# Softmax tiles on VectorE, taken in pairs instead of one at a time

## Chip, cores, metric

The kernel runs on one core of a Trainium2 chip. The metric is the device time of one execution in microseconds (us). ScalarE is called ACT in the profile, VectorE DVE, TensorE PE (its weight loads PEld), GpSimd POOL, SyncE (which issues the DMAs) SP.

## What is computed

Two layers of the same transformer block are run one after the other on x of 2048 rows and 448 columns (bf16); both layers share their weights.

```python
def _A_ref(x, wqkv, wo):
    B, S, D = x.shape
    H = 16; Dh = D // H
    ...                                   # q, k, v of x @ wqkv
    scores = jnp.einsum("bhqd,bhkd->bhqk", q, k) * scale
    p = _softmax(scores, axis=-1)
    o = jnp.einsum("bhqk,bhkd->bhqd", p, v)
    return ... @ wo
def _B_ref(x, w1, b1, w2, b2):
    h = jnp.einsum("bsd,df->bsf", x, w1) + b1
    r = jnp.where(h > zero, h, zero)
    out = jnp.einsum("bsf,fd->bsd", r * r, w2) + b2
x = A_x
x = x + _A_ref(_layernorm(x), A_wqkv, A_wo)
x = x + _B_ref(_layernorm(x), B_w1, B_b1, B_w2, B_b2)
...                                       # the same two lines once more
```

There are 16 heads of width 28 and an MLP of width 1792 with a squared ReLU. The exponentials of the scores, 2 x 16 x 2048 x 2048 of them, are the largest single piece of elementwise work.

## The kernel before

**Tiles.** The rows are cut into blocks of 256 queries (the last two of the second layer have 128). A *pass* is one block and one group of four heads; it runs over the keys in pieces. A *unit* is 512 columns of scores of one head (128 keys on the partitions, 2 x 256 or 4 x 128 columns). There are 2048 units. `s_stream` takes three units at a time as a *group*: PE computes their scores into a PSUM tile `sc` of 1536 columns (two such buffers), L817. `e_stream` lets ScalarE take exp of the tile into `pt` (bf16, NPT = 11 buffers), L842. `p_stream` multiplies `pt` with the values, L1000, and accumulates a pass in one PSUM bank; after it come the softmax division, the output projection, the layer norm and the MLP of the block (`chain`), which are interleaved with the passes of later blocks. Evictions of all these products (L1184, L1191, L1136, L580, L576 and others) run on VectorE, L1242 is filling work for PE.

**Order.** Nothing is scheduled by the chip or a compiler here: a `Planner` with a clock for each engine and an estimated duration for each operation runs generators ("streams") with priorities, always takes the operation that can start earliest, and emits the instructions in that order. Each engine then runs its instructions in the order of emission and waits for semaphores.

**VectorE's share of the exponentials.** For some groups, `apart` decides that VectorE computes the exponential of one of the three units. Then ScalarE's instruction has only 1024 columns. VectorE's way takes five instructions on 512 columns, in a *set* of work tiles:

- L900: scores (PSUM) to a whole number in fixed point (`i`), a scale and a clamp; after it, and after ScalarE, the score buffer is free;
- L916: from the upper half words of `i`, the power of two (`e`);
- L923: from the lower half words and `e`, the first factor, into `e`;
- L928: from the lower half words, the second factor, into `h`;
- L938: their product, into a bf16 tile `pd` that PE reads like `pt`.

There are two sets (`R_v`): the tiles v_i, v_e, v_h, and room in the keys buffer `K_sb` of the other layer (there `h` lies in `i`, so that L928 must wait for L923). The second set is used where that buffer is idle: blocks 2 to 6 in the first layer, all of the second. The `pd` tiles come from `R_pd` (`pd_free`): a tile of its own, idle room in `V_sb`, and, late, NHP buffers of the pool `h`.

`apart` gives a unit to VectorE only if a set is free, `pd` tiles are left, the scores' inputs are there, VectorE was booked for no more than BUSY of the last SPAN = 6 us, and the tile work not yet booked (`left`, 2.74 for one tile) with VectorE's backlog is at most TB us:

```python
if pl.load(SPAN, "DVE") > (LOW if behind(i) else BUSY):
    return None
if max(0.0, pl.clock["DVE"] - now) + left[0] > (TB2 if behind(i) else TB):
    return None
```

`behind(i)` says whether the MLP work is late against a straight line (constants L0E, L0N, L1E, L1N, MARGIN); then the smaller limits LOW and TB2 hold. STOP = 80: none of the last 80 units is given to VectorE. The first step of a tile has a high priority (C_PRIO), the other four (`a_rest`) a low one (V_PRIO, V_LATE, V_LAST as the tile ages), behind the evictions (EV).

Of the kernel before, what the change touches and what calls it, by code (L numbers as in the profile page):

```python
# [18 lines left out]
G = 4  # L19
# [11 lines left out]
OVER = 0.08  # L31
QUICK = 0
QUICK3 = 2
# [7 lines left out]
HALF = 320  # L41
L0E = 1310
L0N = 7.8
L1E = 2020
L1N = 6.6
MARGIN = 4.0
LOW = 0.95
# [10 lines left out]
AHEAD = (range(0, 4), range(0, 4), range(0, 4), range(0, 1))  # L58
SLACK = 0.5
WINDOW = 2.8  # L60
C_PRIO = 1.6
V_PRIO = 8.0
V_LATE = 4.6
V_LAST = 3
V_AGE = 8
V_PAST = 4
OWN3 = 0
FIRST = 50
V_FIRST = 9
V_WAIT = 3.5  # L70
NEAR = 6
FAR = 17
KEEP = 5
LAG = 7
LEAD = 15
LAST = 690
BUSY = 1.0
TB = 4.8
TB2 = 0.3
SPAN = 6  # L80
# [4 lines left out]
MORE = 3  # L85
HEAT = 0.76
HWIN = 3.4
# [3 lines left out]
HOLD1 = 7  # L91
SOON = 0
NHP = 3
THIRD = 1
NL = 0
NLP = 4.9
STOP = 80
HSTOP = 0
CHUNK = 2
EV = 2.9  # L100
CUTS = (0, 10, 16)
# [124 lines left out]
def kernel(  # L226
# [466 lines left out]
    def behind(i):  # L693
# [3 lines left out]
        return done[l] < (min(i, b) - a) / (b - a) * n * per[l] - MARGIN  # L697
    pending = [0]
    left = [0.0]

# [7 lines left out]

    def apart(i, now, us, soon=SOON):

        if len(units) - i < STOP or not LEAD <= len(gbuf) <= LAST:
            return None
        l, qb = passes[units[i][0]][:2]
        if sum(r.when() is not None and r.when() <= now + soon for r in sets_of(units[i])) <= (0 if soon else pending[0]):
            return None
        j = i
        if i + LAG > ends_at[units[i][0]]:
            j = ends_at[units[i][0]] + 1
            while j in taken:
                j += 1  # L720
            if j >= len(units):
                return None
            rows = {u[3] for u in us}
            js = [k for k in range(j, j + 4) if k < len(units) and k not in taken and units[k][3] not in rows]
            j = js[0] if js else j
        if passes[units[j][0]][0] != passes[us[0][0]][0]:
            return None
        if held[0] + 1 > min(sum(r.n for r in pd_free(units[k])) for k in (i, j)):
            return None
        if any(pl.tok.get(d) is None or pl.tok[d].end + LAT["DVE"] > now for d in needs(units[j])):  # L730
            return None
        if pl.load(SPAN, "DVE") > (LOW if behind(i) else BUSY):
            return None
        if max(0.0, pl.clock["DVE"] - now) + left[0] > (TB2 if behind(i) else TB):
            return None
        return j
# [16 lines left out]
    def s_stream():  # L753
        while at[0] < len(units):
# [5 lines left out]
            def fn(e, gi=gi, us=us, js=js):  # L760
# [5 lines left out]
                def next_at(j):  # L766
# [3 lines left out]
                    return rest  # L770
                own, j = True, None
                if OWN3 and bank_free(o.start) and next_at(js[-1] + 1):
                    j = apart(at[0], o.start, us)
                elif len(us) == 3 and THIRD:
                    own = False
                    next_at(js[1] + 1)
                    j = apart(at[0], o.start, us[:2], 0.0)
                if j is None:
                    next_at(js[-1] + 1)
                else:  # L780
                    if not own:
                        us, ks = us[:2], ks[:2]
                        gbuf[gi]["n"] = 2
                    us, ks = us + [units[j]], ks + [3]
                    taken.add(j)
                    held[0] += 1
                    pending[0] += 1
                    next_at(at[0])
                    if own:
                        x = gbuf[gi]["x"] = Op("PE", 0.0, None)  # L790
                        x.res = min((r for r in R_m if r.when() is not None), key=lambda r: r.when())
                        x.turn = len(x.res.rel)
                        x.res.rel.append(None)
                        dst.append(bank(x, "mt"))
                    else:
                        x = gbuf[gi]["x"] = o
                        o.need = 2
                    pl.spawn(C_PRIO, a_unit(gi, x, dst[-1], us[-1], passes[us[0][0]][0]))
                for k, (pi, kb, r, hh) in zip(ks, us):
# [72 lines left out]

    v_i = const.tile([P, 512], DT.int32, name="v_i")
    v_e = const.tile([P, 512], DT.int32, name="v_e")
    v_h = const.tile([P, 512], DT.float32, name="v_h")

    def set_of(res, l):

        k = R_v.index(res)
        two = lambda a: a.rearrange("p (a n) -> p a n", a=2)  # L880
        if k == 0:
            i, e, h = two(v_i[:, :]), two(v_e[:, :]), two(v_h[:, :])
        else:
            keys = K_sb[1 - l][:, :, S - 512:S] if l == 0 else K_sb[0][:, :, 0:512]
            i, e = keys[:, 0:2, :].bitcast(DT.int32), keys[:, 2:4, :].bitcast(DT.int32)
            h = i.bitcast(DT.float32)
        return i, e, h, two

    def a_unit(gi, x, src, unit, l):
        yield Op("-", 0.0, None, deps=[("s", gi)])  # L890
        box = {}

        def take(e):
            pending[0] -= 1
            box["i"], box["e"], box["h"], two = set_of(c.res, l)
            box["two"] = two
            halves = box["i"].bitcast(DT.uint16).rearrange("p a (n t) -> p a n t", t=2)
            box["f"] = halves[:, :, :, 0]
            box["n"] = box["i"].bitcast(DT.int16).rearrange("p a (n t) -> p a n t", t=2)[:, :, :, 1]
            t = nc.vector.tensor_scalar(out=box["i"], in0=two(src), scalar1=EXP_BIAS,  # L900
                                        scalar2=EXP_LOW, op0=ALU.add, op1=ALU.max)
            if x is gbuf[gi]["s"]:
                apart_from(gi, t)
        c = Op("DVE", 0.69, take, deps=[("s", gi)], acq=sets_of(unit), rel=x)
        left[0] += 2.74
        yield c
        left[0] -= 0.6
        pl.spawn(lambda now: V_LAST if e_now[1] - gi >= V_AGE or at[0] > ends_at[unit[0]] + V_PAST else V_LATE if now > c.end + V_WAIT else V_PRIO if gi > FIRST else V_FIRST, a_rest(gi, c, box, unit))

    def a_rest(gi, c, box, unit):  # L910

        root, lin, low = EXP_POLY
        flt = lambda k: box[k].bitcast(DT.float32)

        def power(e):
            nc.vector.tensor_scalar(out=box["e"], in0=box["n"], scalar1=2.0 ** 22, scalar2=EXP_BASE,  # L916
                                    op0=ALU.mult, op1=ALU.add)
        p = Op("DVE", 0.42, power, deps=[c])
        yield p
        left[0] -= 0.34  # L920

        def first(e):
            nc.vector.scalar_tensor_tensor(out=flt("e"), in0=box["f"], scalar=root, in1=flt("e"),  # L923
                                           op0=ALU.add, op1=ALU.mult)
        g = Op("DVE", 0.684, first, deps=[p])

        def square(e):
            nc.vector.scalar_tensor_tensor(out=box["h"], in0=box["f"], scalar=lin, in1=box["f"],  # L928
                                           op0=ALU.add, op1=ALU.mult)
        alone = c.res is R_v[0]  # L930
        h = Op("DVE", 0.684, square, deps=[c] if alone else [c, g])
        for k in (h, g) if alone else (g, h):
            yield k
            left[0] -= 0.6

        def close(e):
            pd = gbuf[gi]["pd"] = pd_of(o)
            nc.vector.scalar_tensor_tensor(out=box["two"](pd), in0=box["h"], scalar=low, in1=flt("e"),  # L938
                                           op0=ALU.add, op1=ALU.mult)
        o = Op("DVE", 0.683, close, deps=[g, h], acq=lambda: pd_free(unit), rel=c, sets=("x", gi))  # L940
        gbuf[gi]["x"] = o
        yield o
        left[0] -= 0.6

# [5 lines left out]
    def p_stream():  # L950


        for pi, (l, qb, g, kbs, first, last) in enumerate(passes):
# [18 lines left out]
            while todo:  # L972
                now = [kb for kb in todo if done(kb)][:some]
                if len(now) < min(some, len(todo)):
                    kb = next(kb for kb in todo if not done(kb))
                    if ("u", pi, kb) not in pl.tok or any(k < 3 and ("e", gi) not in pl.tok for gi, k, _ in where[pi, kb]):
                        yield from got(kb)
                        continue
                    if (e_now[1] - min(gi for gi, _, _ in where[pi, kb]) < NPT - KEEP and e_now[1] < len(gbuf) - 1
                            and len(todo) > len(now) + 1):  # L980
                        yield Op("-", 0.0, None, deps=[("e", e_now[1] + 1)])
                        continue

                    now = sorted(now[:some - 1] + [kb])
                    yield Op("-", 0.0, None, deps=[("x", gi) for gi, k, _ in where[pi, kb] if k == 3])
                todo = [kb for kb in todo if kb not in now]
# [30 lines left out]
            def ev(e, box=box, first=first, last=last, g=g, res=res, n=n, l=l, qb=qb):  # L1017
# [5 lines left out]
                else:  # L1023
                    dst = part(l, qb, g)
                if first:
                    nc.vector.tensor_copy(out=dst, in_=src)
# [266 lines left out]
```

## Time and profile before

| | |
|---|---|
| median of 8 runs | 875.2 us (874.33 to 876.95) |
| profiled execution | 875.5 us, its span 873.7 us |
| ACT, DVE, PE busy | 857.2, 824.0, 828.1 us |
| granted PE clock | 1.000 |
| groups of exponentials on ACT | 509 of 1536 columns, 174 of 1024 |
| tiles on VectorE | 173: 98 in v_i, 75 in K_sb |

The page of the profile lists engines with their busy time, the share of the span and the number of instructions. A row of a group reads: line, engine, operation, out<-in with the shapes, count, then busy time and mean length of one in ns, then the engine's idle time just before these instructions and who ended it. A row of the waits reads: who waited, for whom, us in total, times, longest. A row of the timeline reads: start, length, engine, line, operation. A row of a stretch gives the length, then the busy times of PE, PEld, DVE, ACT and POOL with their instructions, the granted clock, the DMAs' share and GB/s. The instructions of an engine overlap slightly, so that lengths add up to more than the busy time.

### The profile page before, as it was taken

What the parts mean: (1) busy time and instruction counts of PE and PEld (TensorE: products, weight loads), DVE (VectorE), ACT (ScalarE), POOL (GpSimd) and SP (SyncE); (2) the same over time, 40 slices, a digit from 0 to 9 for tenths busy, and PEclk for the clock granted to TensorE, in tenths of its full rate; (3) what the DMA queues carried; (4) which work ended last, traced back from release to release, by engine and by line L of the source; (5) the groups of instructions that cost most, each with busy time, mean ns of one, the idle gap of its engine ahead of it and who ended that gap; (6) DMA issues with size and microseconds to landing.
All of it is one profiled execution on the core that took longest, in us unless ns stands there. A gap on an engine that the chain in (4) does not pass through costs nothing.

```text
span 873.7 us, 28872 instructions
## 1 busy us (share of the span) xinstructions
PE 828.1 (95%) x12673; PEld 445.2 (51%) x12673; DVE 824.0 (94%) x1685; ACT 857.2 (98%) x702; POOL 45.4 (5%) x95
## 2 busy tenths in 40 slices
PE   8999999999999999999999999999999999999998
PEld 5455554454545555454545544444454554545656
DVE  7999899999999999998989999999999999999954
ACT  8999999999999999999999999999999999999995
POOL 3100000001000000100000000000000000000000
DMA  9100100000000000000000000010000000000000
GB/s 256 52 2 3 25 17 15 14 15 15 7 10 15 14 15 15 2 15 14 2 3 2 2 3 2 16 28 27 23 17 26 14 26 25 11 17 15 14 8 18
DMA packets 31514, 17.86 MB, mean 20 GB/s; under 512 B 17242, under 2 KB 30939, under 8 KB 31388
## 3 DMA queue, kind: packets, MB, share of 16 engines
q1 hardware_dynamic: 31388, 16.02, 6.5%
q8 instruction: 99, 1.62, 0.7%
q14 instruction: 27, 0.22, 0.1%
HBM read 13.73 MB, written 2.06 MB: 18 GB/s over the span
## 4 chain that ended last, share of the span: by engine, by line
ACT 59%; PE 19%; issue 10%; DVE 10%; POOL 0%; DMA 0%; DVEq 0%; ACTq 0%
ACT pt L842 59%; PE mt L558 8%; PE sc L817 6%; PE oT L1000 3%; DVE K_sb L923 1%; PE sc L558 1%; DVE r L1184 1%; PE mt L1242 1%; DVE K_sb L928 1%; DVE v_h L928 1%; DVE K_sb L900 1%; DVE v_i L900 1%; DVE x_sb L1136 1%; PE mt L340 1%; DVE v_e L923 1%
## 5 line engine op out<-in xcount | busy, mean ns | idle before, releaser
L842 ACT ACTIVATE pt<-sc 128x1536 bf16<-128x1536 f32 (+1 forms) x683 | 844.9, 1480 | 3.3 <-PE sc L817 3.0
L817 PE MATMUL sc<-Q_sb,K_sb 32*128 32x256 bf16 (+1 forms) x5660 | 317.2, 265 | 32.6 <-ACT pt L842 28.3
L817 PEld LDWEIGHTS <-K_sb 32*128 32x128 bf16 x5660 | 144.1, 92 | 213.3 <-issue 177.1
L1000 PE MATMUL oT<-pt,V_sb 128*32 128x256 bf16 (+1 forms) x3994 | 152.9, 268 | 0.2
L558 PE MATMUL mt<-xnT,w 128*128 128x256 bf16 (+1 forms) x912 | 121.6, 270 | 2.4 <-DVE r L1184 0.7
L1000 PEld LDWEIGHTS <-V_sb 128*32 128x32 bf16 x4352 | 90.9, 96 | 47.4 <-issue 44.6
L558 PEld LDWEIGHTS <-w 128*128 128x128 bf16 x952 | 77.6, 98 | 39.9 <-issue 31.4
L1184 DVE TENSOR_SCALAR r<-mt 128x512 bf16<-128x512 f32 x107 | 72.8, 681 | 5.1 <-PE mt L558 4.8
L900 DVE TENSOR_SCALAR v_i<-sc 128x512 int32<-128x512 f32 x98 | 66.8, 681 | 4.3 <-PE sc L817 3.8
L558 PE MATMUL mt<-w,V_sb 128*128 128x448 bf16 (+1 forms) x288 | 68.1, 348 | 0.0
L928 DVE SCALAR_TENSOR_TENSOR v_h<-v_i 128x512 f32<-128x512 uint16 x98 | 66.5, 678 | 0.0
L923 DVE SCALAR_TENSOR_TENSOR v_e<-v_i,v_e 128x512 f32<-128x512 uint16 x98 | 66.3, 677 | 0.0
L1242 PE MATMUL mt<-xn,ident 128*128 128x448 bf16 x176 | 60.2, 356 | 1.8 <-DVE oTn L1085 0.5
L475 POOL TENSOR_TENSOR ve<-mv,eps_t 128x2 f32<-128x2 f32 (+1 forms) x34 | 13.0, 383 | 814.5 <-DVE mv L453 814.5
L900 DVE TENSOR_SCALAR K_sb<-sc 128x512 int32<-128x512 f32 x75 | 51.1, 682 | 1.9 <-PE sc L817 1.4
L923 DVE SCALAR_TENSOR_TENSOR K_sb<-K_sb 128x512 f32<-128x512 uint16 x75 | 51.3, 683 | 0.8
L928 DVE SCALAR_TENSOR_TENSOR K_sb<-K_sb 128x512 f32<-128x512 uint16 x75 | 50.9, 679 | 0.5
L1136 DVE TENSOR_TENSOR x_sb<-x_sb,mt 128x448 bf16<-128x448 bf16 (+1 forms) x63 | 38.0, 604 | 10.1 <-PE mt L558 9.8
L916 DVE TENSOR_SCALAR v_e<-v_i 128x512 int32<-128x512 int16 x98 | 40.7, 415 | 0.3
L448 DVE BATCH_NORM_STATS2 st<-x_sb 128x6 f32<-128x448 bf16 x64 | 39.0, 612 | 0.7 <-DMA x_sb<-in_A_x_dram 0.7
L558 PEld LDWEIGHTS <-V_sb 128*128 128x128 bf16 x302 | 25.3, 98 | 25.6 <-issue 10.5
L938 DVE SCALAR_TENSOR_TENSOR V_sb<-v_h,v_e 128x512 bf16<-128x512 f32 x55 | 37.4, 680 | 0.2
(102 smaller groups left out, 802.3 us busy)
## 6 DMA issues: line engine op xcount, KB each, us to landing
rec<-scr SPq DMA_DIRECT2D x54, 128.0 KB
x_sb<-in_A_x_dram SPq DMA_DIRECT2D x8, 224.0 KB
out_dram<-x_sb SPq DMA_DIRECT2D x15, 112.0 KB
w<-in_B_w_dram SPq DMA_DIRECT2D x1, 1568.0 KB
w<-in_B_w_dram SPq DMA_DIRECT2D x1, 1344.0 KB
dn<-oT_sb SPq DMA_DIRECT2D x54, 4.0 KB
V_sb<-in_A_wqkv_dram SPq DMA_DIRECT2D x4, 168.0 KB
scr<-dn SPq DMA_DIRECT2D x27, 8.0 KB
```

The lines of the kernel that those rows point to most:

```text
L448: nc.vector.bn_stats(out=box["st"][:, :], in_=x_sb[:, t0 + j, :])
L558: nc.tensor.matmul(box["t"][:, c0:c0 + n], lhsT=lhsT() if callable(lhsT) else lhsT, rhs=rhs, start=a, stop=b)
L817: nc.tensor.matmul(dst[k][:, i * nt * P:(i + 1) * nt * P], lhsT=K_sb[l][rows, g, (kb + i) * P:(kb + i + 1) * P], rhs=Q_sb[rows, g, t0 * P: ...
L842: t = nc.scalar.activation(out=pt[:, 0:n], in_=gbuf[gi]["sc"][:, 0:n], func=AF.Exp, scale=float(np.log(2.0)) * 2.0 ** -FRAC)
L900: t = nc.vector.tensor_scalar(out=box["i"], in0=two(src), scalar1=EXP_BIAS, scalar2=EXP_LOW, op0=ALU.add, op1=ALU.max)
L916: nc.vector.tensor_scalar(out=box["e"], in0=box["n"], scalar1=2.0 ** 22, scalar2=EXP_BASE, op0=ALU.mult, op1=ALU.add)
L923: nc.vector.scalar_tensor_tensor(out=flt("e"), in0=box["f"], scalar=root, in1=flt("e"), op0=ALU.add, op1=ALU.mult)
L928: nc.vector.scalar_tensor_tensor(out=box["h"], in0=box["f"], scalar=lin, in1=box["f"], op0=ALU.add, op1=ALU.mult)
L1000: nc.tensor.matmul(box["t"][DHP * hh:DHP * hh + DHP, 0:n], lhsT=V_sb[l][:, kb + i, 4 * g + hh, :], rhs=p[:, c0:c0 + n], start=begin and kb ...
L1136: nc.vector.tensor_tensor(out=x_sb[:, tb, lo:hi], in0=x_sb[:, tb, lo:hi], in1=t[:, 0:hi - lo], op=ALU.add)
L1184: nc.vector.tensor_scalar(out=r[:, 0:w], in0=t[:, 0:w], scalar1=0.0, scalar2=None, op0=ALU.max)
L1242: nc.tensor.matmul(t[:, 0:D], lhsT=ident[:, :], rhs=xns[0][:, 0:D], start=True, stop=True)
```

## The change

Tiles for VectorE are now collected in pairs. `apart` opens a *box* with a first tile; the next group tries to join a second one to it (`joins`, without asking for VectorE's load or backlog). Each tile keeps an L900 step and an L938 step of its own on 512 columns; the exponent (L916) and the two factors (L923, L928) run once on 1024 columns for both. They start when the second tile's scores are in, or, when the next group can't join, for the first alone. The set v_i, v_e is twice as wide; v_h is gone, the second factor goes into `i`. The set in K_sb is twice as wide where `room` says so. A set is free again after the second close. NHP goes from 3 to 2. `p_stream` may now take other key pieces while one waits for a tile of VectorE. Further constants of the giving out, of priorities and of filling work are changed; QUICK decides for which head groups of the last block but one the division goes by transposes on VectorE (`norm_turn`) or by DMAs through DRAM (`norm_pair`).

```diff
-QUICK = 0
+QUICK = 4
+WIDE = 4
-L0E = 1310
-L0N = 7.8
-L1E = 2020
-L1N = 6.6
-MARGIN = 4.0
+L0E = 1300
+L0N = 7.4
+L1E = 1980
+L1N = 6.4
+MARGIN = 3.0
...
-V_PRIO = 8.0
-V_LATE = 4.6
+V_PRIO = 7.0
+V_LATE = 3.8
...
-BUSY = 1.0
-TB = 4.8
-TB2 = 0.3
+BUSY = 0.98
+TB = 2.1
+TB2 = 0.6
...
-HEAT = 0.76
+HEAT = 0.64
...
-SOON = 0
-NHP = 3
+SOON = 0.6
+NHP = 2
...
-STOP = 80
+STOP = 40
...
-    def apart(i, now, us, soon=SOON):
+    def apart(i, now, us, soon=SOON, joins=False):
...
+        if joins:
+            return j
         if pl.load(SPAN, "DVE") > (LOW if behind(i) else BUSY):
...
+                j, box, open_box = None, None, opened.pop() if opened else None
+                if len(us) == 3:
                     next_at(js[1] + 1)
-                    j = apart(at[0], o.start, us[:2], 0.0)
+                    if open_box and open_box["c"][0].res is not None and (open_box["c"][0].res is R_v[0] or room(...) and ...):
+                        j = apart(at[0], o.start, us[:2], 0.0, True)
+                        box = open_box
...
+                    if j is None:
+                        box = {"c": [], "gi": [], "unit": []}
+                        j = apart(at[0], o.start, us[:2], 0.0)
+                if open_box and box is not open_box:
+                    pl.spawn(rank(open_box), a_rest(open_box, 1))
...
+                    if box is open_box:
+                        pl.spawn(C_PRIO, a)
+                        pl.spawn(rank(box), a_rest(box, 2))
...
-    v_i = const.tile([P, 512], DT.int32, name="v_i")
-    v_e = const.tile([P, 512], DT.int32, name="v_e")
-    v_h = const.tile([P, 512], DT.float32, name="v_h")
+    v_i = const.tile([P, 2, 512], DT.int32, name="v_i")
+    v_e = const.tile([P, 2, 512], DT.int32, name="v_e")
...
+    def room(unit):
+        l, qb, *_ = passes[unit[0]]
+        return not parts_left[l] and (l == 1 or qb <= WIDE)
...
-        p = Op("DVE", 0.42, power, deps=[c])
+        p = Op("DVE", 0.15 + n * 0.267, power, deps=list(box["c"]))
...
-        g = Op("DVE", 0.684, first, deps=[p])
+        g = Op("DVE", 0.15 + n * 0.534, first, deps=[p])
...
-        h = Op("DVE", 0.684, square, deps=[c] if alone else [c, g])
+        h = Op("DVE", 0.15 + n * 0.534, square, deps=[*box["c"], g])
+        yield h
+        for k in range(n):
+            gi, unit = box["gi"][k], box["unit"][k]
+            def close(e, k=k, gi=gi):
...
+            o = Op("DVE", 0.683, close, deps=[g, h], acq=lambda unit=unit: pd_free(unit), rel=box["c"][0] if k == n - 1 else None, sets=("x", gi))
...
+                    old = min((gi for b in todo for gi, k, _ in where.get((pi, b), ()) if k < 3), default=e_now[1])
                     if (e_now[1] - min(gi for gi, _, _ in where[pi, kb]) < NPT - KEEP and e_now[1] < len(gbuf) - 1
                             and len(todo) > len(now) + 1):
-                        yield Op("-", 0.0, None, deps=[("e", e_now[1] + 1)])
-                        continue
+                        if e_now[1] - old < NPT - 1:
+                            yield Op("-", 0.0, None, deps=[("e", e_now[1] + 1)])
+                            continue
+                    else:
+                        now = now[:some - 1] + [kb]
```

## The prediction

> **What bounds the kernel now.** I read the page's busy times first, then the waits, then the groups with shapes kept apart, then VectorE's timeline, then busy times by stretch.
>
> ```profile
> PE 828.1 (95%) x12673; PEld 445.2 (51%) x12673; DVE 824.0 (94%) x1685; ACT 857.2 (98%) x702; POOL 45.4 (5%) x95
> ```
> ```profile
> PE sc L817 <- ACT pt L842: 28.3, 87, 0.7
> ...
> ACT pt L842 <- PE sc L817: 3.0, 6, 1.1
> ```
> ScalarE (ACT) is busy for 857.2 of 873.7 us, and its exponentials wait only 3.0 us for scores, while the scores wait 28.3 us for it. PE and VectorE are nearly full too, but ScalarE sets the pace: in the timeline its first exponential starts at 10.6 us and its last ends at 858.6, and the end takes 15.1 us more. So the span is 10.6 + 848.0 + 15.1.
>
> ```profile
> L842 ACT ACTIVATE pt<-sc 128x1536 bf16<-128x1536 f32 x509 | 725.2, 1588 | 3.3 <-PE sc L817 3.0
> ...
> L842 ACT ACTIVATE pt<-sc 128x1024 bf16<-128x1024 f32 x174 | 199.4, 1165 | 0.0
> ```
> There are always 683 groups of three tiles. Where VectorE takes a group's third tile, the exponential has 1024 columns and is 1.588 - 1.165 = 0.423 us shorter. That is the exchange rate of this change: **one tile more or fewer on VectorE is 0.423 us of the end**, as long as ScalarE is never kept waiting. VectorE has 173 tiles now (98 in the set v_i, 75 in the set in K_sb).
>
> ```profile
> L900 DVE TENSOR_SCALAR v_i<-sc 128x512 int32<-128x512 f32 x98 | 66.8, 681 | 4.3 <-PE sc L817 3.8
> L928 DVE SCALAR_TENSOR_TENSOR v_h<-v_i 128x512 f32<-128x512 uint16 x98 | 66.5, 678 | 0.0
> L923 DVE SCALAR_TENSOR_TENSOR v_e<-v_i,v_e 128x512 f32<-128x512 uint16 x98 | 66.3, 677 | 0.0
> ...
> L916 DVE TENSOR_SCALAR v_e<-v_i 128x512 int32<-128x512 int16 x98 | 40.7, 415 | 0.3
> ```
> A fifth step, L938, takes 0.68 us. These are durations; instructions overlap their neighbours, so what a step costs is the distance between starts:
>
> ```profile
> 306.12 0.68 DVE L923 SCALAR_TENSOR_TENSOR K_sb<-K_sb 128x512 f32<-128x512 uint16 x1
> 306.84 0.69 DVE L928 SCALAR_TENSOR_TENSOR K_sb<-K_sb 128x512 f32<-128x512 uint16 x1
> 307.45 0.68 DVE L900 TENSOR_SCALAR v_i<-sc 128x512 int32<-128x512 f32 x1
> 308.05 0.41 DVE L1026 COPY oT_sb<-oT 128x256 f32<-128x256 f32 x1
> 308.38 0.68 DVE L938 SCALAR_TENSOR_TENSOR V_sb<-K_sb 128x512 bf16<-128x512 f32 x1
> 308.98 0.42 DVE L916 TENSOR_SCALAR v_e<-v_i 128x512 int32<-128x512 int16 x1
> 309.32 0.68 DVE L928 SCALAR_TENSOR_TENSOR v_h<-v_i 128x512 f32<-128x512 uint16 x1
> ```
> L900 to its unrelated successor: 0.60 us. L923 to the L928 that has to wait for it: 0.72, so a dependent neighbour costs 0.12 more. The 256-column copy takes 0.33. Hence 256 columns cost 0.27 and an instruction 0.07 beside them. A tile without such waits is 4 x 0.60 + 0.34 = 2.74 us; the mean over the starts of all 157 tiles between 120 and 820 us is 2.84, because two tiles are usually interleaved and fill each other's waits.
>
> ```profile
> 200.00:300.00 100.00, 94.98 (x1401) 50.28 (x1392) 98.86 (x197) 99.70 (x82) 4.39 (x10) 1.00 0.05 13
> ...
> 800.00:850.00 50.00, 47.83 (x1103) 29.46 (x1104) 40.27 (x94) 50.00 (x40) 2.05 (x4) 1.00 0.03 10
> ```
> The third busy time is VectorE's: 98.9 of 100 us in the middle, 40.3 of 50 near the end, since its last tile starts at 819.9 (STOP = 80 units before the end). From 120 to 820 us, 445 us go to tiles and some 36% to the other work.
>
> **The change part by part.** *Wide steps.* Two tiles now need two L900 steps (1.20), one exponent step on 1024 columns, two factor steps on 1024 and two closing steps (1.20). No row shows a factor step on 1024 columns: from 2 x 0.60 = 1.20 (nothing saved) down to 4 x 0.267 + 0.07 = 1.14; I take 1.14, as the 256- and 512-column rows lie on that line. The exponent step runs at twice the rate already; the 1024-column bf16 copy at L510 (0.677 long, 0.60 from start to start) is its nearest row. The sum is 1.20 + 0.60 + 2.28 + 1.20 = 5.28 against 2 x 2.74 = 5.48: 0.20 us for two tiles. Waits: exponent, first factor, second factor (in place now, so always after the first) and close hang on one another, 4 x 0.12 = 0.48 for a pair with nobody between; other work falls between perhaps half of them, so I take 0.24 (ends 0 and 0.48). That makes 5.52 a pair, 2.76 a tile against 2.84. Over 157 tiles this is 12.6 us or 4.6 tiles; I take +5, ends -3 and +12.
>
> The Trainium skill says in "VectorE: DVE Perf Modes", section "The DRAIN you can't avoid", that the next instruction does not start before the pipe has emptied. The starts above contradict it: 0.60 apart with 0.68 long instructions. By the page's rule the three instructions saved in a pair would be worth about 0.44 us, my estimate from its rule and the 0.68, twice what the starts give.
>
> *Giving out.* A pair is opened only if the tile work queued on VectorE and its backlog are below TB = 2.1 us (4.8 before, where a whole second tile could be queued), if VectorE was at most 98% booked over the last 6 us, and it starts its wide steps only when the partner's scores are there, one group (0.92 to 1.35 us) later. The rule opens the next pair at the earliest when the second factor step starts; then 1.14 + 1.20 + 0.60 (the next pair's first step) = 2.94 us of tile work are left, which with 36% other work last 4.6 us. The next pair's exponent step can start after a mean wait for a group of 0.7, the scores 0.5, the partner 1.35 and its L900 0.6: 3.2 us, or 4.5 if one opening is refused. On the mean VectorE doesn't run dry, but where the other work is thin, or an opening is refused, it does. I put 0.15 us on each of 86 pairs, 13 us or 4.5 tiles (ends 0 and 13).
>
> *Narrow places.* The K_sb set is one tile wide for blocks 5 and 6 of the first layer and until the second layer's partial sums are gone (13 parts, 416 units at 2048/848 = 2.4 a us, some 170 us). There a tile goes alone, is released one group later and is one chain. NHP goes from 3 to 2: at most 5 tiles may be held late instead of 6, and held tiles live longer as pairs. Together I take -6 tiles, ends 0 and -12. In the opening, where only one set exists and VectorE idles 1 to 3 us in 20, the wide set can give +2; I count that in the +5's upper end.
>
> *STOP 40.* Forty units more at 2.4 a us are 17 us more in which tiles are given out. VectorE took 5 tiles per 20 us before; the block of MLP evictions stays, so +3 (0 to 5). QUICK = 4 replaces four short chains of transposes (L1069 to L1085, about 1.1 us each) by evictions and a DMA round trip (the queue of SP) for the last block but one; by the timeline its MLP's first products start behind the previous block's, at 851.7 us, while its attention's last scaling ends at 833.5. The round trip is hidden by these 17 us; without that cover it would cost about 5 us, the time of the three DMAs.
>
> *Tiles in all:* 173 + 5 - 4.5 - 6 + 3 = 170.5; every refusal counts against it and I round down to 169: 4 x 0.423 = +1.7 us.
>
> *ScalarE's waits.* The scores' buffer is free when both ScalarE and L900 have read it. L900 can now stand behind a 1.22 us instruction instead of a 0.68 us one, and two groups of 1024 columns follow each other at every pair (13 times now), which leaves PE 0.92 us instead of 1.35 for the next scores. Behind L900 the next group's score matmuls and the other evictions are queued. ScalarE's starts now come late by 4.8 us in all, 16 times over 0.04; I add 0.8, ends 0 and 5.
>
> *Sum:* the profiled execution has 875.5 us (span 873.7 and 1.8 around it). 875.5 + 1.7 + 0.8 = 878.0; the median of the runs shown is 0.3 lower: **877.7**.
>
> **The rivals.** *VectorE fills up* (faster): pairs have few waits, the rules bind seldom, the last 17 us give 5 tiles: 178 to 186 tiles, -2 to -5.5 us, and the end stays: 869.5 to 873.4. For it: VectorE has been at 98.9% and each pair is cheaper. It decides once more than about 6 tiles are gained over what ScalarE's waits take. *ScalarE waits* (much slower): L900 stands behind wide steps often enough to delay the scores at 86 pairs by 0.06 to 0.1 us and the tile count falls by 5 to 15: 881.5 to 887. Against it: PE has 28.3 us of slack before the scores. *Nothing moves*: gains and losses cancel, or pairs seldom find a partner and tiles go singly: 873.5 to 877.
>
> **How the numbers follow.** About 0.2%, 1.75 us, is what a measurement of this kernel can tell from no change. Forecast (876.9 to 881.5, at 877.7): 0.37. ScalarE waits: 0.11. Cancel: 0.15. VectorE fills up: 0.37. Faster is the last, 0.37; same 0.15; slower 0.48. The forecast's own range is 876.9 to 881.5; since cases of both signs hold most, the full range goes from 870.0 into the fast case to 884.0 into the slow one.
>
> **What would show it.** Right: fewer than 173 exponentials with 1024 columns; wide factor steps of 1.21 to 1.22 us, 3 fewer instructions in a pair; VectorE's share between 120 and 820 us a per cent or two lower; ScalarE's idle time before L842 a little over 3.3 us; last tile about 835; the last exponential to the end still about 15 us. Wrong: 178 or more groups of 1024 columns, or a time below 873, would say that the cheaper pair went into tiles; ScalarE idle over 8 us, that the wide steps hold up the scores; an end over 17 us, that the DMA round trip wasn't hidden.

## The result

The changed kernel takes 878.8 us (median of 10 runs, 877.8 to 880.1) against 875.4 for the kernel before (28 runs): a ratio of 1.0036, interval 1.0028 to 1.0044. A second chip gave 1.0025 (1.0015 to 1.0036; run a_again below). It is slower by 2 to 3.4 us, as forecast (877.7).

The lines that answer to those of before. The page's busy times, then the waits (who waited, for whom, us, times, longest):

```profile
PE 819.1 (93%) x13012; PEld 456.2 (52%) x13012; DVE 802.8 (92%) x1446; ACT 860.3 (98%) x704; POOL 44.3 (5%) x95
```
```profile
PE sc L826 <- ACT pt L851: 44.7, 125, 0.7
...
ACT pt L851 <- PE sc L826: 4.4, 7, 1.1
```

ScalarE is still the pace, and busy for 3.1 us more. VectorE has become emptier by 21 us. The groups with shapes kept apart:

```profile
L851 ACT ACTIVATE pt<-sc 128x1536 bf16<-128x1536 f32 x514 | 719.3, 1612 | 3.8 <-PE sc L826 3.7
...
L851 ACT ACTIVATE pt<-sc 128x1024 bf16<-128x1024 f32 x169 | 183.2, 1198 | 0.7 <-PE sc L826 0.7
...
L908 DVE TENSOR_SCALAR v_i<-sc 128x512 int32<-128x512 f32 x105 | 71.6, 682 | 8.2 <-PE sc L826 7.3
L945 DVE SCALAR_TENSOR_TENSOR v_e<-v_i,v_e 128x1024 f32<-128x1024 uint16 x48 | 58.5, 1219 | 0.8
...
L938 DVE TENSOR_SCALAR v_e<-v_i 128x1024 int32<-128x1024 int16 x48 | 32.8, 684 | 0.5
```

VectorE has 168 tiles, 5 fewer: 105 in v_i and 63 in K_sb. 136 of them form 68 pairs (48 and 20 wide steps), 32 went alone. (The group of 1024 columns has one instruction more, the last group of two units; before, too.) Busy times by stretch:

```profile
200.00:300.00 100.00, 94.24 (x1421) 51.25 (x1420) 93.51 (x160) 100.00 (x82) 4.49 (x10) 1.00 0.05 13
...
800.00:850.00 50.00, 47.15 (x1178) 30.88 (x1170) 44.00 (x83) 50.00 (x41) 1.24 (x2) 1.00 0.06 13
```

VectorE's 98.9 us of 100 have become 93.5; near the end it has more, as tiles now go on to 831 us.

**Where the 3.5 us of the two profiled executions (873.7 to 877.2) are.** In the trace, a full group takes 1.343 us from end to end and one of 1024 columns 0.917, so a tile is 0.426 us. Five tiles are 2.1 us. ScalarE's starts that come over 0.04 us late add up to 4.5 us before and 5.4 after: 0.9. From the last exponential to the end it is 15.1 before (858.6 to 873.7) and 15.7 after (861.6 to 877.2): 0.6. The first exponential starts 0.1 earlier. (The mean lengths in the rows above, 1612 and 1198 ns, contain the overlap of one instruction with the next, so they are no measure of the pace.) 1.4 of the 5.4 us of late starts follow a stretch of 3.4 us in which PE had half its clock; the last section is on these.

### The profile page after: what moved, and what is told of

It is laid out like the page before. It is cut to its first block, busy times and chain, and to the rows that moved or that the text cites. A ratio compares the mean times of both kernels' runs of the same rounds, so it can differ in the third digit from the quotient of the medians.

```text
span 877.2 us, 29304 instructions
## 1 busy us (share of the span) xinstructions
PE 819.1 (93%) x13012; PEld 456.2 (52%) x13012; DVE 802.8 (92%) x1446; ACT 860.3 (98%) x704; POOL 44.3 (5%) x95
## 4 chain that ended last, share of the span: by engine, by line
ACT 64%; PE 18%; issue 10%; DVE 6%; DMA 0%; POOL 0%; SPq 0%; ACTq 0%
ACT pt L851 64%; PE mt L559 8%; PE sc L826 6%; PE oT L1031 3%; PE sc L559 1%; DVE K_sb L945 1%; DVE V_sb L965 1%; DVE v_i L952 1%; DVE K_sb L908 0%; DVE v_i L908 0%; DVE v_e L945 0%; DVE x_sb L1168 0%; DMA V_sb<-in_A_wqkv_dram 0%; DVE K_sb L952 0%; DVE st L449 0%
## 5 line engine op out<-in xcount | busy, mean ns | idle before, releaser
L826 PEld LDWEIGHTS <-K_sb 32*128 32x128 bf16 x6136 | 166.7, 92 | 224.1 <-issue 184.8
L908 DVE TENSOR_SCALAR v_i<-sc 128x512 int32<-128x512 f32 x105 | 71.6, 682 | 8.2 <-PE sc L826 7.3
L1216 DVE TENSOR_SCALAR r<-mt 128x512 bf16<-128x512 f32 (+1 forms) x107 | 72.6, 678 | 5.6 <-PE mt L559 5.1
L559 PE MATMUL mt<-w,V_sb 128*128 128x448 bf16 x274 | 68.3, 355 | 0.0
L945 DVE SCALAR_TENSOR_TENSOR v_e<-v_i,v_e 128x1024 f32<-128x1024 uint16 (+1 forms) x57 | 64.6, 1134 | 0.9
L952 DVE SCALAR_TENSOR_TENSOR v_i<-v_i 128x1024 f32<-128x1024 uint16 (+1 forms) x57 | 64.5, 1132 | 0.6
L908 DVE TENSOR_SCALAR K_sb<-sc 128x512 int32<-128x512 f32 x63 | 43.0, 683 | 7.7 <-PE sc L826 7.2
L965 DVE SCALAR_TENSOR_TENSOR V_sb<-v_i,v_e 128x512 bf16<-128x512 f32 x65 | 43.3, 677 | 0.1
L1168 DVE TENSOR_TENSOR x_sb<-x_sb,mt 128x448 bf16<-128x448 bf16 x63 | 38.4, 609 | 5.4 <-PE mt L559 5.4
L945 DVE SCALAR_TENSOR_TENSOR K_sb<-K_sb 128x512 f32<-128x512 uint16 (+1 forms) x43 | 40.0, 930 | 0.7
L952 DVE SCALAR_TENSOR_TENSOR K_sb<-K_sb 128x512 f32<-128x512 uint16 (+1 forms) x43 | 39.7, 924 | 0.5
L938 DVE TENSOR_SCALAR v_e<-v_i 128x1024 int32<-128x1024 int16 (+1 forms) x57 | 36.6, 642 | 0.6
L1031 PE MATMUL oT<-V_sb,V_sb 128*32 128x256 bf16 (+1 forms) x202 | 34.4, 274 | 0.0
```

The costliest lines, as they stand in the source:

```text
L559: nc.tensor.matmul(box["t"][:, c0:c0 + n], lhsT=lhsT() if callable(lhsT) else lhsT, rhs=rhs, start=a, stop=b)
L826: nc.tensor.matmul(dst[k][:, i * nt * P:(i + 1) * nt * P], lhsT=K_sb[l][rows, g, (kb + i) * P:(kb + i + 1) * P], rhs=Q_sb[rows, g, t0 * P: ...
L908: t = nc.vector.tensor_scalar(out=i, in0=src if box["most"] == 2 else src.rearrange("p (a n) -> p a n", a=2), scalar1=EXP_BIAS, scalar2=EX ...
L938: nc.vector.tensor_scalar(out=row(box["e"]), in0=high_half(), scalar1=2.0 ** 22, scalar2=EXP_BASE, op0=ALU.mult, op1=ALU.add)
L945: nc.vector.scalar_tensor_tensor(out=flt("e"), in0=low_half(), scalar=root, in1=flt("e"), op0=ALU.add, op1=ALU.mult)
L952: nc.vector.scalar_tensor_tensor(out=flt("i"), in0=low_half(), scalar=lin, in1=low_half(), op0=ALU.add, op1=ALU.mult)
```

## The experiments

Clock figures are the mean granted clock of a run. The experiments ran on three chips, and a ratio is against the kernel before on the same chip; its medians there are 877.4 us (a_busy1, a_singles, a_narrow, a_stop80), 875.9 (a_again, a_oldconsts, b_newconsts, b_stop40) and 875.9 (the others). Idle and busy time of VectorE are between 120 and 820 us, from the starts and ends in the traces.

**a_again**, the changed kernel once more.

> The changed kernel itself, beside the others on one chip. In the runs so far its time has two levels, 877.8 to 878.2 us where the mean granted clock is 1.000 and 878.8 to 879.0 where it is 0.998, that is, where one stretch of 3.4 us has half the clock. Both are expected again, about 1.1 us apart; kernel before and changed kernel, both at 1.000, should be 2.4 us apart: 5 tiles x 0.426 = 2.1, the rest at the end.

Both levels came: at 1.000 7 of 12 runs, 877.7 to 878.0; at 0.998 four, 878.9 to 879.2; one at 0.996, 880.2. The kernel before, on the same chip, has 13 of 17 at 1.000, median 875.9. At 1.000 the two are 1.9 us apart (2.4 expected), of which 2.1 would be the tiles; what the half clock adds is in the last section.

**a_busy1**: one limit of the giving out as before.

```diff
-BUSY = 0.98
+BUSY = 1.0
```

> The changed kernel with BUSY = 1.0 as before the change (0.98), all else as changed; 182 tiles are emitted for VectorE instead of 168. Theory 1 (only the number of tiles counts, the tighter rule lost them): 14 x 0.426 = 6.0 us less, about 873 us. Theory 2 (the rule protects a date: the second layer's first passes need the last keys of the first layer's last block, which are evicted by VectorE at about 548 to 550 us, and ScalarE waits there for 0.8 us already): more tiles push that eviction, ScalarE waits there for over 10 us, 888 to 898 us, and the end after the last exponential grows as well.

893.9 us, ratio 1.019 (1.017 to 1.021): theory 2. ScalarE's and VectorE's rows of the timeline around 550 us:

```profile
541.26 3.53 ACT L851 ACTIVATE pt<-sc 128x1024 bf16<-128x1024 f32 x3
560.12 1.02 ACT L851 ACTIVATE pt<-sc 128x1024 bf16<-128x1024 f32 x1 [15.33 <-PE sc L826]
```
```profile
549.89 0.61 DVE L1168 TENSOR_TENSOR x_sb<-x_sb,mt 128x448 bf16<-128x448 bf16 x1
...
553.85 0.70 DVE L526 TENSOR_SCALAR xn<-x_sb,mv,rstd 128x448 bf16<-128x448 bf16 x2 [1.08 <-POOL rstd L477]
555.37 0.69 DVE L511 COPY xnT<-tp 128x1024 bf16<-128x1024 bf16 x1 [0.82 <-PE tp L499]
558.02 0.69 DVE L581 CAST K_sb<-mt 128x512 bf16<-128x512 f32 x1 [1.96 <-PE mt L559]
```

ScalarE stands for 15.33 us until the scores come, and the chain behind it is read from below: scores need the key tile that L581 evicts at 558.0; that needs the transposed, normalised rows (L511, L526); those need the last sum of the MLP (L1168). The first layer's MLP wasn't finished when the second layer asked for its keys. 182 tiles had gained ScalarE 6 us, one wait took 15, and the time from the last exponential to the end grew from 15.7 to 22.1 us (869.3 to 891.4). PE ran at half its clock from 554.1 to 560.9 us, behind a standstill of its own, so that a part of the 15 us is that. The same place in the changed kernel and in the kernel before:

```profile
548.93 0.68 DVE L581 CAST K_sb<-mt 128x512 bf16<-128x512 f32 x1
```
```profile
550.17 3.71 ACT L851 ACTIVATE pt<-sc 128x1024 bf16<-128x1024 f32 x3 [0.72 <-PE sc L826]
```
```profile
527.07 0.68 DVE L580 CAST K_sb<-mt 128x512 bf16<-128x512 f32 x1
```

The kernel before had its keys 22 us earlier. The changed kernel meets the date with nothing to spare (0.72 us of idle ScalarE), with 104 tiles started by 548 us against 108.

**a_oldconsts**: the changed code with all constants of before but NHP.

> The changed code with every constant as before (but NHP = 2): 189 tiles are emitted, 16 more than before the change and 21 more than in the changed kernel. Theory 1 (a tile more is 0.426 us less): about 868.5 us. Theory 2 (VectorE's other work must meet the date at which the second layer needs its last keys, and the end): the last K_sb evictions of the first layer come at 565 us or later, ScalarE waits 20 to 40 us in all, over 900 us.

908.2 us, ratio 1.036 (1.034 to 1.039): theory 2 again, with 189 tiles.

```profile
ACT pt L851 <- PE sc L826: 30.6, 24, 5.9
```

ScalarE waits for scores 24 times, 30.6 us, the longest 5.9 at 560 us; the keys' evictions there are at 558.9 and 565.7. From the last exponential (883.8) to the end it takes 22.1 us. So pairs under the old limits win 16 tiles over the kernel before (3 before 120 us, 7 from there to 820 us, 6 behind that, where everything is late), 6.8 us, and it ends 32 us later all the same.

**b_newconsts**: the code before with all constants of the changed kernel.

> The code before with every constant as in the changed kernel, tiles one at a time: 158 tiles are emitted, 15 fewer than before. If the tighter rule is what takes the tiles away, and pairs win 10 back under it, ScalarE's last exponential ends 15 x 0.426 = 6.4 us later than before, at 865 us, its waits stay under 5 us, and the time is 882 to 886 us, according to whether the end grows because tiles now go on up to 838 us. If pairs are what loses the tiles, this kernel is near the time before, 875 to 878.

884.2 us, ratio 1.009 (1.007 to 1.011). The two groups of exponentials:

```profile
L842 ACT ACTIVATE pt<-sc 128x1536 bf16<-128x1536 f32 x524 | 748.5, 1614 | 1.9 <-PE sc L817 1.8
L842 ACT ACTIVATE pt<-sc 128x1024 bf16<-128x1024 f32 x159 | 189.7, 1197 | 0.0
```

158 tiles, a last exponential at 862.7 (865 had been expected; ScalarE's late starts are only 2.3 us), then 18.9 us. **The changed constants take 15 tiles from the old code; pairs win 10 of them back.**

**a_singles**: the changed kernel, never joined.

```diff
-if open_box and open_box["c"][0].res is not None and (...):
+if False and open_box and open_box["c"][0].res is not None and (...):
```

> The changed kernel without joining: each tile goes alone, in sets and limits as changed; 160 tiles are emitted. If pairs are worth something at these limits, it is slower than the changed kernel by 8 x 0.426 = 3.4 us, about 882 us, with VectorE idle for longer than the changed kernel's 41 us between 120 and 820 us. If pairing itself costs the time (L908 behind long instructions, groups of 1024 columns in a row), ScalarE's late starts (5.6 us in the changed kernel) shrink and the time is that of the changed kernel, 877 to 879, or less.

881.5 us, ratio 1.0046 (1.0031 to 1.0061), 160 tiles: pairing is worth 8 tiles at these limits, 3.4 us by the price of a tile. (At a clock of 1.000 it is 5.1 us over the kernel before on its chip, the changed kernel 1.9 on another.) VectorE is idle for 42.3 us there and 40.9 in the changed kernel, so the gain isn't idle time but cheaper tiles: from start to start, idle left out, 2.86 us a tile alone and 2.76 in pairs. Over 147 tiles that is 14 us, the five tiles by which 142 and 147 differ between 120 and 820 us; the other three lie before 120 us (14 against 17). ScalarE's late starts did shrink, 3.1 us against 5.4, but that is less than the tiles lost.

**a_narrow**: pairs, but exponent and factors on 512 columns, the two tiles interleaved.

```diff
+for k, row in enumerate(parts):      # parts: the two halves of the set
+    ps.append(Op("DVE", 0.42, power, deps=[box["c"][k]]))
+    ...
+for k, row in enumerate(parts):      # the same for first and square
+    gs.append(Op("DVE", 0.684, first, deps=[ps[k]]))
```

> The changed kernel with pairs as they are, but exponent and factor steps run on 512 columns for each tile, interleaved (first tile, second tile, first tile ...), so three instructions more in a pair and no waits between neighbours; 163 tiles are emitted. The term of the prediction (0.20 us saved a pair by wide instructions, 0.24 lost by waits that interleaving hides) says that wide and narrow cost the same: within 1 us of the changed kernel apart from 5 x 0.426 = 2.1 us for the tiles, 880 to 882. If the wide instructions hold up L908 and the evictions, ScalarE's late starts fall below 4 us and the time is below 879. If wide instructions save more than that, VectorE's start-to-start time on a tile rises from 2.88 to over 2.95 us and the time is above 882.

885.3 us, ratio 1.008 (1.006 to 1.010); one of its four runs had the clock at 1.000, 882.6, the others were at 0.996, the profiled one with two stretches of half clock. 163 tiles, 2.77 us each without idle time (2.76 wide), 2.92 with it: the steps cost the same, as the term said. The time is above the 880 to 882 that I gave, at a clock of 1.000 by little. ScalarE is late by 7.8 us in the profiled execution; without the 3.0 us that the run at 1.000 is shorter some 5 are left, an estimate, and not under 4: nothing here says that wide instructions hold it up. The order of all the other work moved too (idle 51 us), so that what the wide steps alone are worth in us isn't settled by this run.

**a_stop80**: `STOP = 80` in the changed kernel.

> The changed kernel with STOP = 80 as before the change (40); 166 tiles are emitted, the instructions before some 820 us are the same. The prediction gave STOP = 40 three tiles; here it is two, 0.85 us: 879.7 us if nothing else moves, or no difference if the end takes up the change. The granted clock fell to 0.69 between 105 and 110 us in the changed kernel's profile, with 1.7 us of late starts at 107 to 112 us: as the instructions there are the same, the dip is there again if it belongs to the order of the work, and not if it was an accident of that execution (then these starts are late by 0.4 us or less).

879.4 us, ratio 1.0025 (1.0014 to 1.0035) on another chip, whose kernel before had 877.4. 9 of its 12 runs are at 1.000, median 879.2, 2.7 us over the runs of before at 1.000 there (13 of 19, median 876.4); the changed kernel was 1.9 over. The difference of 0.8 us is what two tiles give. The stretch of half clock was not at 107 us but at 166, and of the 1.7 us of late starts at 107 to 112 us only 0.4 are left. So the order of the work alone doesn't fix its place; a_again's trace has it at 107 us again (last section).

**b_stop40**: `STOP = 40` in the kernel before.

> The kernel before with STOP = 40 alone: 178 tiles are emitted, 5 more. The prediction priced this at 0.42 us less a tile, the work beside it staying where it is: 875.2 - 2.1 = about 873 us on the first chip, or 2.1 us below the kernel before on this one. The rival: VectorE's evictions at the end are due as well, so the last exponential ends 2.1 us earlier but the 15.1 us after it grow by more than that: 2 to 5 us slower than before.

881.9 us, ratio 1.006 (1.004 to 1.008): the rival. 178 tiles, the last exponential ends at 855.5, 3.1 us earlier, and the end comes 23.0 us after it, not 15.1. ScalarE's rows of the timeline:

```profile
848.92 6.61 ACT L842 ACTIVATE pt<-sc 128x1536 bf16<-128x1536 f32 x5
...
864.92 0.60 ACT L1182 ACTIVATE r<-mt 128x512 bf16<-128x512 f32 x1 [5.77 <-PE mt L558]
```

**a_quick0**: `QUICK = 0` in the changed kernel.

> The changed kernel with QUICK = 0 as before the change: the last block but one divides by transposes on VectorE. 170 tiles are emitted (+2, -0.85 us). The prediction says that QUICK = 4 costs nothing, so this is 877 to 878 us. If the transposes and the tiles given out up to 838 us get in the way of the last evictions, the last exponential ends earlier, but the time after it grows from 15.7 us to over 20, as in the kernel before with STOP = 40, and the time is 881 to 885 us.

885.0 us, ratio 1.010 (1.009 to 1.012). 170 tiles, and 22.8 us from the last exponential (861.9) to the end (884.8), with the same wait:

```profile
871.34 0.60 ACT L1214 ACTIVATE r<-mt 128x512 bf16<-128x512 f32 x1 [5.77 <-PE mt L559]
```

In both, the end is 7 to 8 us longer, with a wait of ScalarE's of 5.77 us for a product of PE; the longest wait at the end is 3.74 us in the kernel before and 2.36 in the changed one. PE isn't idle meanwhile: in a_quick0 it is busy all through that wait, mostly with products of the MLP, and for 19.9 of the last 23.2 us, in the changed kernel for 12.7 of the last 15.6. So work of PE's had been left over. In the changed kernel with STOP = 40, QUICK = 4 is worth these 7 us. Whether QUICK = 0 would do with STOP = 80 there wasn't run.

**a_fill**: more to do for PE, order of the work kept.

```diff
+extra = int(gi > 40 and pl.load(HWIN) + 0.22 * again / HWIN < FILL)    # FILL = 0.76
-for i in list(range(4)) * (again + 1):
+for i in list(range(4)) * (again + 1 + extra):
```

> The changed kernel with the same order of work, but 159 groups whose surroundings leave PE below 76% booked repeat their score matmuls once more (6 matmuls, some 0.2 us, into the same buffer; the result is not changed). If the half-clock stretches of 3.4 us follow stretches in which PE had too little to do (the lowest 3.4 us stretches of the changed kernel have PE busy for 0.64 to 0.66, those of the kernel before 0.71 or more), runs with a mean clock of 0.998 or 0.996 vanish here and all runs lie at the upper level's 877.7 to 878.2 us. If they are an accident of the execution, about half of the runs are at 0.998 again, 1.1 us slower. The extra matmuls themselves may cost 0 to 1 us where they delay the scores.

890.2 us, ratio 1.016 (1.015 to 1.018). All five runs are at 1.000 and lie within 0.3 us of each other: the half clock is gone. But the extra matmuls cost far more than the 0 to 1 us I gave them: ScalarE is late by 15.8 us instead of 5.4, in 75 starts, nearly all by less than 0.6 us. The filling was in the way of the scores.

**b_more** and **a_more**: further constants of the two codes. Both set QUICK = 3, and this has a consequence that I had not foreseen: the fourth head group of the last block but one goes by transposes, and the third waits for it as a partner for its DMAs and never gets one. So both kernels leave out that block's output projection and MLP (63 sums into x_sb instead of 65), and their times are not those of the whole work.

> The code before, one tile at a time, with other constants of the giving out (BUSY 1.02 in the first layer and 1.005 in the second, TB 5.0 and 4.6, LOW 0.96, the straight lines of the MLP work moved, priorities and STOP = 72): 177 tiles are emitted, 4 more than before. If the dates are still met (no wait of ScalarE at 548 us, 15 us after the last exponential), 4 x 0.426 = 1.7 us less than the kernel before on this chip, some 874 us; if not, at least as slow as before.

> The changed code with pairs, with a few constants moved (QUICK 3, FIRST 90, FAR 17, HOT 0.86, HOLD1 6): 171 tiles are emitted, 3 more than in the changed kernel and 2 fewer than before the change. 3 x 0.426 = 1.3 us less than the changed kernel, 876.5 us; if pairs could match the time before at all, it would be here.

b_more: 872.1 us, ratio 0.995 (0.994 to 0.997), 177 tiles, last exponential at 855.4. a_more: 878.3 us, ratio 1.002 (1.000 to 1.004), 171 tiles, last exponential at 858.4, its runs spread from 875.2 at a clock of 1.000 to 882.6 at 0.988. What can be read, with care, since some of the missing work would have been done beside the last 20 us of it, is ScalarE's stretch: in b_more it is 844.2 us from the first exponential (11.1) to the last, in the kernel before 848.0, and the keys' evictions at 542.8 still meet their date. Whether the old code with 177 tiles and all its work would be faster stays open, as does a version that beats both; neither was tried.

## Why the prediction was right, step by step

*The price of a tile.* 0.423 us was predicted, 0.426 measured, and the sums above close with it.

*Wide steps.* The factor step on 1024 columns is 1.22 us long and 1.13 to 1.15 from start to start (predicted 1.14), the exponent step 0.684 and 0.60 (0.60). VectorE's timeline:

```profile
645.08 0.68 DVE L938 TENSOR_SCALAR K_sb<-K_sb 128x1024 int32<-128x1024 int16 x1
645.68 0.42 DVE L1223 TENSOR_TENSOR V_sb<-r 128x512 bf16<-128x512 bf16 x1
...
646.61 1.21 DVE L945 SCALAR_TENSOR_TENSOR K_sb<-K_sb 128x1024 f32<-128x1024 uint16 x1
647.75 0.42 DVE L1223 TENSOR_TENSOR V_sb<-r 128x512 bf16<-128x512 bf16 x1
```
```profile
105.94 0.68 DVE L938 TENSOR_SCALAR v_e<-v_i 128x1024 int32<-128x1024 int16 x1
106.65 1.22 DVE L945 SCALAR_TENSOR_TENSOR v_e<-v_i,v_e 128x1024 f32<-128x1024 uint16 x1
107.80 0.68 DVE L1159 TENSOR_TENSOR oTn<-oT_sb,rec 128x512 bf16<-128x512 f32 x1
```

With other work between, a wide exponent step costs 0.60; with its own factor step next, 0.71 to 0.72. The latter is the case in 45 of the 90 exponent steps between 120 and 820 us, wide and narrow (29 of the 59 wide ones): at this one of four places, the half that I had assumed. The measured cost of a tile, 2.76 us, is the predicted one to the digit.

*But the gain worked out from it was wrong.* I set 2.76 against 2.84 for the kernel before, and that figure contained VectorE's idle time behind tile steps while mine did not. (It has 158 tiles in that stretch, not 157, so 2.82.) Without idle time the kernel before has 2.763, the changed one 2.758: the five tiles of this term aren't there in the changed kernel. They aren't nothing either. With the old constants on both sides a tile costs 2.763 us alone and 2.70 in pairs (a_oldconsts), some 11 us or 4 tiles over 165, with 136 of the 189 tiles in pairs; there only 13 of 56 wide exponent steps have their own factor step next. With the new constants on both sides it is 2.83 (b_newconsts) or 2.86 (a_singles) alone and 2.76 in pairs. So pairs make a tile cheaper by 0.06 to 0.10 us, the new constants make it dearer by as much, and I had worked with one of the two. That the old code lost little to waits because it had two tiles in hand, which the smaller TB no longer allows, fits these figures, but was not tried alone. Nor is it the wide steps by themselves: two tiles interleaved in narrow steps cost 2.77 (a_narrow).

*Giving out.* Here lies the loss, and the sum of two terms was right: -4.5 for running dry and -6 for narrow places were predicted, and 147 tiles instead of 158 lie between 120 and 820 us. VectorE's idle time there rose from 13.2 to 40.9 us; 27.7 us are 10 tiles at 2.76. The forecast's own sign was a share of VectorE a per cent or two lower; it fell by four, from 98.1 to 94.2. The division between the two terms was wrong as far as the runs tell. a_oldconsts has the same narrow places and the old constants, and VectorE is idle for 16.5 us and has 165 tiles there; b_newconsts has no narrow set and the new constants, and is idle for 55.1 us with 139 tiles. So it is the limits that leave VectorE without tiles, twice the 13 us that I put on them for 86 pairs (68 came), and the -6 for narrow places isn't borne out: that both together came to the measured loss is luck. In the old code the same constants cost 15 tiles.

*The opening and STOP.* Before 120 us the changed kernel has 17 tiles and the kernel before 15, the +2 that I had left out of the sum; 4 start after 820 us where +3 was predicted, of which STOP by itself gives 2. *QUICK* was said to cost nothing because a round trip is hidden; the end grew by only 0.6 us, which agrees, but that it was needed I had missed: without it the end is 7 us longer.

*The tiles in all:* -11 + 2 + 4 = -5, for a forecast of -4. The forecast had +5 for cheaper tiles that the new constants took away, made up for by the opening, by a tile more late and by 1.5 of rounding down. That the total came within one tile is luck, for its parts did not.

*ScalarE's waits.* +0.8 predicted, +0.9 measured in the profiled executions, by luck and not from the predicted place. (The prediction read 4.8 us of late starts in the kernel before; by the median pace it is 4.5.) Of the 5.4 us, 1.9 are at the very beginning in both kernels, 0.9 are the second layer's date (548 to 550 us), 0.4 a start at 107 us that is late in a_stop80's trace too, and 1.4 the next two starts, behind the half clock; the other 0.9 at three places weren't traced. Without the half clock 4.0 us are left (a_stop80 gives the same), half a us less than in the kernel before, with 68 neighbouring groups of 1024 columns instead of 13. So at full clock the term has the wrong sign, and L908 behind wide steps cost at most those 0.9 us.

*The time.* The four runs of the changed kernel at a clock of 1.000 have a median of 877.9 us, 0.2 from the forecast. The median of all ten lies 0.9 higher through the half clock, for which the prediction had no term.

*The rival "VectorE fills up"* fell, and a_busy1 and a_oldconsts show why: its premise, that filling VectorE is free, is false. The tiles came (182 and 189, where it spoke of 178 to 186), and the time went up by 1.9 and 3.6 per cent. I had read 98.9% as room in reserve for tiles; the work that fills VectorE has dates, at 550 us and at the end. That the tighter limits are there for these dates is shown; why pairs need them tighter than single tiles is argued only: a second tile joins without being asked for load or backlog, so tiles come in twos when the MLP is late. That was not tried alone. *ScalarE waits* fell too: its starts are late by 5.4 us, where over 8 of idle time would have spoken for it. *Nothing moves* fell as well: 878.8 and 878.0 us lie outside its 873.5 to 877.

## What to carry to other kernels

An engine that is busy for 99% can be filled with work of two kinds, work that somebody waits for and work that pays by the piece; before adding to the second, find the dates of the first (here the first use of the second layer's keys) and how many us it has to spare. What fewer, longer instructions save depends on what hides their waits: compare both sides with the same treatment of idle time and with the same constants, or the gain of one and the loss of the other can't be told apart. And when constants are changed with the code, run both crosses, new code with old constants and old code with new ones: they took a difference of 5 tiles apart into -15 for the constants and +10 for the pairs, or, the other way round, into +16 for the pairs and -21 for the constants.

## What the runs showed of the hardware

The granted clock of PE falls to one half for stretches of 3.4 us without PE having stood still. Busy times of the changed kernel by stretch (PE's first, the clock third from the right):

```profile
100.00:105.00 5.00, 4.93 (x80) 2.80 (x78) 4.18 (x8) 5.00 (x5) 0.00 (x0) 1.00 0.20 57
105.00:110.00 5.00, 4.48 (x51) 2.77 (x48) 3.44 (x6) 4.65 (x4) 0.00 (x0) 0.69 0.13 40
```

From 106.9 us on the clock was 0.5 for 3.4 us. Two of ScalarE's starts behind it are late by 1.4 us in all, and a run with one such stretch (mean clock 0.998) takes 1.0 to 1.3 us longer. The changed kernel had at least one in 6 of 10 and 5 of 12 runs, a_stop80, whose order of work is the same up to some 820 us, in 3 of 12, and the kernel before in 6 of 19, 4 of 17 and 4 of 17. 14 of 34 against 14 of 53 can be chance: that the change made it more frequent isn't shown.

Its place changes from run to run, but not freely: 106.9 us in the changed kernel and 107.2 in a_again, 166.4 in a_stop80 and 166.2 in a_quick0, where a second stretch begins 201.4 us later, 59 times 3.413. In a_busy1 PE stands still for a whole 3.4 us, and the half clock follows at once (columns as above):

```profile
550.64:554.05 3.41, 0.00 (x0) 0.00 (x0) 2.23 (x6) 0.00 (x0) 1.06 (x4) 1.00 0.00 0
554.05:557.46 3.41, 2.38 (x15) 1.83 (x16) 1.19 (x3) 0.00 (x0) 0.00 (x0) 0.50 0.02 5
```

In the changed kernel PE was at work in the 3.4 us ahead: busy for 0.83 of them ahead of the stretches at 107 us, for 0.65 ahead of those at 166. The filling work for PE is down from HEAT = 0.76 to 0.64: the emptiest 3.4 us of the changed kernel have PE busy for 0.64, those of the kernel before for 0.71. With a_fill's repeated scores none of five runs has the half clock, which speaks for too little work on PE as the cause. It isn't shown, and a bound can't be given: stretches with PE busy for 0.61 (b_newconsts, from 841.9 us) and 0.59 (a_more, from 792.4) had no half clock behind them.

The Trainium skill, "TensorE: Matmul & The Clock Gate", section "What's actually happening", tells of a free-running window of 3.4 us, after which a PE that was idle gets half the clock. The length and the multiples of it agree with the rows here, and so does a_busy1. But the section speaks of an idle window, and PE's longest gap in the changed kernel between 20 and 850 us is 0.7 us.

Taking the counts of the two kernels as they are, this is some 0.2 to 0.3 us on average (half of the runs against a quarter to a third, at 1.1 us each), beside the 2 us of the tiles. In a median it can be more: on the first chip, where six of the changed kernel's ten runs had it, it is 0.9 us, and that is most of the difference between the 3.4 us there and the 2.0 on the second.
